# Attention jobs of the third chunk on re-spaced to eight half steps, and the first chunk's jobs put in a written order

## The chip, the cores and the metric

One core of a Trainium2 chip. The metric is the device time of one execution in microseconds (us), lower is better. The kernel before has been timed in three runs, whose median is quoted; one more execution of it was profiled.

## What is computed

Three stages, each feeding the next, all in 32-bit floating point (the reference, cut to what matters):

```python
# q, k, v: 4 batches x 8 heads x 576 positions x 64
mask_plain = (rel >= 0) & (rel < 32)                      # heads 0 to 3
mask_dil = (rel >= 0) & (rel < 128) & (rel % 4 == 0)      # heads 4 to 7
scores = np.where(masks, q @ k^T / 8, -1e9)
attn = np.exp(scores - max); attn /= attn.sum() + 1e-9
x = attn @ v                                              # 2304 tokens x 512
h = x @ w_in;  g = max(h, 0) + alpha * min(h, 0)          # 512 -> 2048
x = g @ w_out                                             # 2048 -> 512
h = x @ w_in2; g = P(h) / (Q(h) + 1e-6)                   # P, Q: small polynomials
out = g @ w_out2
```

The four weight matrices arrive as pairs of 32-bit words (64-bit floats) and are decoded on the chip.

## The kernel before

**Chunks and jobs.** The 2304 tokens are cut into 8 chunks of 288 (number u = 0 to 7). Attention for a chunk is 4 jobs, one for each pair of heads `hp` (pairs 0 and 1 plain, 2 and 3 dilated). `attention_job` (L308) is a generator, and each `yield` ends a step: -1 loads queries and keys (`tq`, `tk`); 0 transposes them on TensorE (L382, L386) into `pq`, `pk`; 1 copies these to `qT`, `kT` on ScalarE (L392, L393); 2 loads the values (`tv`); 3 the scores `ps` on TensorE (L423 dilated, L437 plain); 4 and 7 the row maxima of either half on VectorE (L451, into `pr` and `mx`); 6 and 8 the exponentials on ScalarE with their sums (L459); 9 the division by the sums (L466, L467, and the multiply L469, on VectorE for the first three chunks and on GpSimd after); 10 TensorE turns the probabilities (`pp`, L480); 11 ScalarE copies them out (L486); 12 TensorE multiplies by the values (`px`, L531); 13 ScalarE and VectorE write the high and low part of x (`x1h` L543, `x1l` L545).

**The dense layers.** One step n is one chunk u and one block f of 128 of the 2048 hidden columns, and each n has two half steps, built by `half1` (L830): the first holds the 12 matmuls of h (three products of split numbers for each of 4 blocks, L553), the second the 12 matmuls of y for step n-2 (L727). Between them ScalarE computes `r` (L687), VectorE `larger` (L690), ScalarE the high part of g (L693), VectorE the low part (L696). The list `SEQ` says what n is: n = 0 to 7 is chunk 0 with f = 0 to 7 (weights and x whole, in 32 bits, L670), n = 8 to 15 chunk 1 with the same f, n = 16 to 23 chunk 0 with f = 8 to 15, n = 24 to 31 chunk 1 with these, and then each of chunks 2 to 7 has 16 steps in a row.

**Weight decoding** goes in 36 turns, each with its load (L134 for w_in, L139 for w_out, issued by SyncE), a scaling on ScalarE (`w64_exponent`, L148) and, on VectorE, a sign (L154), an upper (L161) and a lower part (L168), and for some a split (L198, L215, L227). Two buffers hold the raw words (`RAWB`). `PACE` sets how many turns a step n takes in.

**What sets the order.** Chunk 0's jobs, the first decode turns and the first steps of chunk 1's first job are called in the order of the string `HEAD` (L72): a digit is the next step of that job, d, x, j, J, i, h, l are a turn's load, scaling, sign, upper, lower, and split parts, k is a step of chunk 1's first job. From there on the half steps call what tables name: `STEPS` gives for each step of a job its half step after the job's start, `BASES` the starts of a chunk's four jobs relative to the 32 half steps of the chunk before, `ON_PE` which steps go behind that half step's matmuls. The first eight jobs (chunks 1 and 2) have starts of their own, `EARLY`, and denser steps, `EARLY_STEPS`. The scheduler of the framework may still move instructions against this order, except inside `tc.manual_schedule()`. Attention has two PSUM banks, and single buffers for `pr`, `qT`, `kT`, `tq`, `tk`.

```python
att_rest.setdefault(s0 + 2, []).append((i + AHEAD, -1))     # the next job's loads
s0 = EARLY[i] if i < len(EARLY) else i // KD * 2 * NF + BASES[i % KD]
```

Of the kernel before, what the change touches and what calls it, by code (L numbers as in the profile page):

```python
# [22 lines left out]
def tile_attention_moe_moe2(  # L23
# [48 lines left out]
    HEAD = '0d12d30011xj01Ji223301h2300110011xj22223333Jil001101d22010331hlxj220133Ji012301d23k0123hl23xj2323Jidhl'  # L72
# [3 lines left out]
    MANH = ''  # L76
    HPS = (1, 0, 3, 2)
    POOLJ = ()
    SPLIT = True
# [7 lines left out]
    PACE = ((8, 0.75), (16, 0.25), (24, 0.75), (128, 0.22))  # L87
# [190 lines left out]
    def mem_head(nm, dil):  # L278

        if dil:  # L280
            at = {"tq": (0, 0), "tk": (0, 512), "tv": (1, 0), "qT": (1, 512),
                  "kT": (2, 0), "pT": (2, 416), "pr": (3, 0)}
        else:
            at = {"tq": (0, 0), "qT": (0, 384), "tv": (1, 0), "kT": (1, 640),
                  "tk": (2, 0), "pr": (2, 512), "pT": (3, 0)}
# [22 lines left out]
    def attention_job(mem, u, hp, bk, eng=nc.sync, split=False):  # L308
# [5 lines left out]
        first = t0 == 0  # L314
        if dil:
            nb, bq = 4, C1 // 4
            kw = bq if first else bq + W
# [3 lines left out]
            tk = mem("tk", [kw, 2, 4 * D])  # L321

            def load(t, src, back):
                n = t.shape[0]
                s0 = t0 if not back or first else t0 - 4 * W
                eng.dma_start(
                    t,
                    src[b, h0 : h0 + 2, s0 : s0 + 4 * n, :].rearrange(
                        "h (i r) d -> i h (r d)", r=4
                    ),  # L330
                )

            load(tq, q, False)
            load(tk, k, True)

            duo = lambda t, j: t[:, j // 2, (j % 2) * 2 * D : (j % 2 + 1) * 2 * D]
            q_rows, k_rows = bq, kw
        else:


            nb, bq = 3, 96
            groups = ((0, 1, 2), (3, 4))
            rows, span = P, 96
            back = 0 if first else W
# [35 lines left out]
        kn = 4 if dil else nk  # L380
        for j in range(nb):
            nc.tensor.transpose(  # L382
                pq[:, j * q_rows : (j + 1) * q_rows], duo(tq, j), ident[:q_rows, :q_rows]
            )
        for j in range(kn):
            nc.tensor.transpose(  # L386
                pk[:, j * k_rows : (j + 1) * k_rows], duo(tk, j), ident[:k_rows, :k_rows]
            )
        yield
        kT = mem("kT", [P, kn * k_rows])  # L390
        qT = mem("qT", [P, C1])
        nc.scalar.activation(qT, pq[:, :C1], AF.Copy)  # L392
        nc.scalar.activation(kT, pk[:, : kn * k_rows], AF.Copy)  # L393
        yield
        if dil:
            tv = mem("tv", [kw, 2, 4 * D])
            load(tv, v, True)
        else:
            tv = mem("tv", [span, 5, 2, D])
            s0 = t0 - back  # L400
            if first:
                load_one(tv[:, 0], v, s0)
                load(tv[:, 1:], v, s0 + key[1], QS, 4)
            else:
                load(tv, v, s0, QS, 5)
# [8 lines left out]
        def scores():  # L414


            if dil:

                ps[:] = [bk(f"ps{nm}_{g}") for g in range(2)]
                for c in range(nb):  # L420
# [36 lines left out]
        def exponentials(g):  # L457
            for j in groups[g]:
                nc.scalar.activation(  # L459
                    pr[:, j, :], pr[:, j, :], AF.Exp, scale=-1.0,  # L460
                    bias=mx[:, j : j + 1], accum_out=sm[:, j : j + 1],
                )

        def norm(gs):
            s = slice(groups[gs[0]][0], groups[gs[-1]][-1] + 1)
            nc.vector.tensor_scalar_add(sm[:, s], sm[:, s], 1e-9)  # L466
            nc.vector.reciprocal(sm[:, s], sm[:, s])  # L467
            n = s.stop - s.start
            (nc.vector if u < NORM_DVE else nc.gpsimd).tensor_tensor(  # L469
                pr[:, s], pr[:, s],  # L470
                sm[:, s].unsqueeze(2).to_broadcast([rows, n, span]), op=ALU.mult,
# [13 lines left out]
        def turned(g):  # L485
            nc.scalar.activation(  # L486
                pT[:, g * width[0] : g * width[0] + width[g]], pp[g][:span, : width[g]],
                AF.Copy,
            )
# [16 lines left out]
        if split:  # L506
            turn(0)
            yield
            turned(0)
            yield  # L510
        rest = (1,) if split else (0, 1)
        norm(rest)
        yield
        for g in rest:
            turn(g)
        yield
        for g in rest:
# [41 lines left out]
    if True:  # L559
# [27 lines left out]
        def x1_tiles(u):  # L587
            if u == 0:
# [42 lines left out]
        nc.gpsimd.dma_start(alpha_sb, alpha.rearrange("(f p) -> p f", p=P))  # L631


        nc.vector.tensor_scalar(side, alpha_sb, 1.0, -2.0, op0=ALU.is_gt, op1=ALU.mult)
        nc.vector.tensor_scalar_add(side, side, 1.0)
        nc.vector.tensor_tensor(salpha, side, alpha_sb, op=ALU.mult)
        nc.gpsimd.dma_start(ab[:, 0:4], a_in.unsqueeze(0).to_broadcast([P, 4]))
        nc.gpsimd.dma_start(ab[:, 4:6], b_in.unsqueeze(0).to_broadcast([P, 2]))
        def head():
            for s in HEAD:  # L640
                if s in stages:
                    stage(s)
# [414 lines left out]
```

## Time and profile before

| what | before |
|---|---|
| three runs, median (lowest to highest) | 957.85 us (955.93 to 959.39) |
| the profiled execution, its own time | 958.93 us |
| its span in the profile | 957.2 us |
| mean granted TensorE clock | 0.981 of full |
| busy: TensorE, VectorE, ScalarE, GpSimd | 931.6, 663.9, 632.3, 213.3 us |

The span is what the profiler records from the first to the last instruction; 1.7 us of the execution lie around it. The dense layers of attention's chunks end at about 546 us; what follows is the third stage, which has no attention. Four stretches are used below: 0 to 43.4 us (the head: chunk 0's attention until the first `larger`, L690, is done), 43.4 to 139.4 (steps up to n = 23), 139.4 to 181.6 (n = 24 to 31), and 181.6 to 546 (chunks 2 to 7).

### The profile page before, as it was taken

The numbers are of one execution on the slowest core, as the hardware profiler recorded it, in microseconds if no ns is written. First come the engines' busy times: TensorE is split into PE (matmuls) and PEld (weight loads), VectorE is DVE, ScalarE is ACT, GpSimd is POOL, SyncE is SP. The second block draws the span as 40 slices with busy tenths as digits, with TensorE's granted clock in tenths as the row PEclk, the third lists the DMA queues.
The fourth block names the chain that finished last, engine by engine and source line by source line (L and its number), as shares of the span: only waits on it lengthen the run. The fifth ranks groups of instructions, "written<-read, shape, count | busy, mean of one in ns | idle before, by whom it ended". The sixth has DMA issues, their size and how long they took to land.

```text
span 957.2 us, 18319 instructions
## 1 busy us (share of the span) xinstructions
PE 931.6 (97%) x6640; PEld 859.2 (90%) x6640; DVE 663.9 (69%) x1578; ACT 632.3 (66%) x1579; POOL 213.3 (22%) x257
## 2 busy tenths in 40 slices
PE   5898999999999999999999999999999999999998
PEld 4677998999999999999999999999999999999996
DVE  3688996556556556556536698877787777777776
ACT  3788676665564565655636588777777767776775
POOL 2000000010000010000103345444344343443432
PEclk7699999999999999999999999999999999999999
DMA  7666444453644534534145412030020020020000
GB/s 167 184 185 195 143 149 141 137 184 104 194 122 114 190 108 141 160 87 132 47 136 174 153 57 67 0 98 2 20 80 1 34 67 1 34 67 1 34 1 33
DMA packets 93898, 94.39 MB, mean 99 GB/s; under 512 B 40176, under 2 KB 81648, under 8 KB 93808
## 3 DMA queue, kind: packets, MB, share of 16 engines
q1 hardware_dynamic: 87360, 83.78, 28.5%
q0 software_dynamic: 6448, 9.45, 4.0%
q8 instruction: 52, 0.85, 0.4%
q14 instruction: 38, 0.31, 0.1%
HBM read 69.48 MB, written 23.72 MB: 97 GB/s over the span
## 4 chain that ended last, share of the span: by engine, by line
PE 81%; DMA 7%; ACT 6%; DVE 3%; issue 1%; SPq 1%; POOL 0%; POOLq 0%; ACTq 0%; DVEq 0%
PE h L553 38%; PE o L970 20%; PE y L727 16%; DMA raw<-in_moe_w_out_dram 5%; PE px L531 2%; DMA raw<-in_moe_w_in_dram 2%; PE pp L480 1%; ACT hd L459 1%; PE ps L423 1%; PE h L670 1%; ACT raw L148 1%; ACT pr L459 1%; DVE h L690 1%; DVE w L161 1%; PE ps L437 1%
## 5 line engine op out<-in xcount | busy, mean ns | idle before, releaser
L553 PE MATMUL h<-x1h,wl 128*128 128x288 f32 x480 | 146.5, 305 | 1.9 <-ACT g_6h L693 1.6
L553 PE MATMUL h<-x1l,wh 128*128 128x288 f32 x480 | 142.4, 297 | 0.0
L553 PE MATMUL h<-x1h,wh 128*128 128x288 f32 x480 | 141.3, 294 | 0.0
L690 DVE SCALAR_TENSOR_TENSOR h<-h,salpha,r 128x288 f32<-128x288 f32 x128 | 66.9, 523 | 96.6 <-ACT r L687 96.2
L553 PE MATMUL h<-x2h,wl 128*128 128x384 f32 x384 | 130.4, 340 | 0.0
L553 PE MATMUL h<-x2h,wh 128*128 128x384 f32 x384 | 130.0, 339 | 0.0
L553 PE MATMUL h<-x2l,wh 128*128 128x384 f32 x384 | 129.6, 338 | 0.0
L469 POOL TENSOR_TENSOR pr<-pr,sm 128x480 f32<-128x480 f32 (+2 forms) x20 | 24.0, 1198 | 448.3 <-DVE sm L467 382.7
L687 ACT ACTIVATE r<-h,side 128x288 f32<-128x288 f32 x128 | 63.7, 498 | 87.1 <-PE h L553 84.9
L902 POOL TENSOR_SCALAR qq<-hh,babs 128x384 f32<-128x384 f32 x96 | 56.9, 593 | 224.8 <-ACT hh L900 224.7
L905 POOL TENSOR_TENSOR qq<-qq,w 128x384 f32<-128x384 f32 x96 | 97.9, 1019 | 8.3 <-POOL qq L902 0.4
L553 PEld LDWEIGHTS h<-x1h,wl 128*128 128x128 f32 x480 | 90.0, 188 | 5.5 <-ACT g_6h L693 2.1
L553 PEld LDWEIGHTS h<-x1l,wh 128*128 128x128 f32 x480 | 90.2, 188 | 0.8 <-DVE x1l L545 0.5
L553 PEld LDWEIGHTS h<-x1h,wh 128*128 128x128 f32 x480 | 90.2, 188 | 0.1
L900 ACT ACTIVATE hh<-h 128x384 f32<-128x384 f32 x96 | 47.1, 490 | 62.2 <-PE h L553 62.2
L907 DVE TENSOR_TENSOR t<-h,t 128x384 f32<-128x384 f32 x96 | 53.5, 558 | 47.2 <-ACT t L906 46.8
L553 PEld LDWEIGHTS h<-x2h,wl 128*128 128x128 f32 x384 | 72.0, 188 | 4.0
L553 PEld LDWEIGHTS h<-x2l,wh 128*128 128x128 f32 x384 | 72.1, 188 | 3.6
L916 ACT ACTIVATE w<-qq 128x384 f32<-128x384 f32 (+1 forms) x98 | 50.9, 519 | 34.0 <-POOL qq L905 33.9
L553 PEld LDWEIGHTS h<-x2h,wh 128*128 128x128 f32 x384 | 72.0, 187 | 0.0
L924 DVE TENSOR_TENSOR qq<-qq,w 128x384 f32<-128x384 f32 (+1 forms) x98 | 54.2, 553 | 25.0 <-ACT w L919 24.7
L459 ACT ACTIVATE pr<-pr,mx 128x96 f32<-128x96 f32 (+2 forms) x182 | 65.0, 361 | 3.8 <-DVE mx L451 3.8
(379 smaller groups left out, 2558.0 us busy)
## 6 DMA issues: line engine op xcount, KB each, us to landing
raw<-in_moe_w_in_dram SPq DMA_DIRECT2D x32, 512.0 KB
raw<-in_moe_w_out_dram SPq DMA_DIRECT2D x32, 512.0 KB
w2f<-w SPq DMA_DIRECT2D x32, 256.0 KB
w<-w2f SPq DMA_DIRECT2D x16, 512.0 KB
x2h<-x2hi POOLq DMA_DIRECT2D x6, 768.0 KB, 5.1
x2l<-x2lo POOLq DMA_DIRECT2D x6, 768.0 KB, 6.6
out_dram<-o SPq DMA_DIRECT2D x15, 256.0 KB
tq<-in_q_dram SPq DMA_DIRECT2D x28, 72.0 KB
```

Of the source, the lines that this page charges most:

```text
L459: nc.scalar.activation(pr[:, j, :], pr[:, j, :], AF.Exp, scale=-1.0, bias=mx[:, j : j + 1], accum_out=sm[:, j : j + 1],)
L553: nc.tensor.matmul(ph[:, :n], lhsT=w_[:, c * P : (c + 1) * P], rhs=x_[:, c, :], start=(i == 0), stop=(i == 3 * KD - 1),)
L687: nc.scalar.activation(r, h, AF.Identity, scale=sg)
L690: nc.vector.scalar_tensor_tensor(h, h, sa, r, op0=ALU.mult, op1=ALU.max)
L727: nc.tensor.matmul(ys[c][:, :C1], lhsT=w_[:, s], rhs=g_, start=begin and i == 0, stop=end and i == 2,)
L900: nc.scalar.activation(hh, h, AF.Square)
L902: nc.gpsimd.tensor_scalar(qq, hh, babs, 1.0 + 1e-6, op0=ALU.mult, op1=ALU.add)
L905: nc.gpsimd.tensor_tensor(qq, qq, w, op=ALU.add)
L907: nc.vector.tensor_tensor(t, h, t, op=ALU.mult)
L916: nc.scalar.activation(w[:, s], qq[:, s], AF.Abs_reciprocal_sqrt, scale=2.0**-44)
L924: nc.vector.tensor_tensor(qq[:, s], qq[:, s], w[:, s], op=ALU.mult)
L970: nc.tensor.matmul(o2[c][i], lhsT=g_, rhs=w_, start=(f == 0 and j == 0), stop=(f == NF - 1 and j == 2),)
```

## The change

The tables of steps and starts are new. A job of chunks 2 to 7 now starts eight half steps after the one before it (-6, 2, 10, 18), and its four TensorE steps lie at half steps 0, 2, 6 and 12 of the job. Only chunk 1's jobs keep the denser early table. `HEAD` is a new string, which runs under `tc.manual_schedule()`. In chunk 0's jobs query and key loads are issued by SyncE and ScalarE in turn, value loads by GpSimd; the copy of `kT` and of the first half of the turned probabilities goes to VectorE; the exponentials no longer add up their rows, which one VectorE reduction for a job does. The division is one step for both halves. The loads of alpha and its three small VectorE operations come late in the head (`a`).

```diff
-    STEPS = (1, 2, 3, 4, 4, 4, 7, 7, 8, 8, 8, 9, 10, 13)
-    ON_PE = (0, 3, 5, 10, 12)
-    BASES = (-3, 3, 9, 15)
+    STEPS = (0, 1, 1, 2, 3, 3, 3, 3, 4, 5, 6, 7, 12, 13)
+    ON_PE = (0, 3, 10, 12)
+    BASES = (-6, 2, 10, 18)
...
-    EARLY = (-6, -2, 1, 5, 40, 48, 55, 58)
+    EARLY = (-6, -2, 1, 5)
...
-    HEAD = '0d12d30011xj01Ji223301h2300110011xj22223333Jil001101d22010331hlxj220133Ji012301d23k0123hl23xj2323Jidhl'
+    HEAD = (
+        '0123dd01010101000001111232212033322220010021333312132xjJid21'
+        '2323hlxjJid333hlaxjJidkhl'
+    )
...
-    PACE = ((8, 0.75), (16, 0.25), (24, 0.75), (128, 0.22))
+    PACE = ((8, 0.85), (16, 0.25), (24, 0.75), (128, 0.22))
...
-        nc.scalar.activation(kT, pk[:, : kn * k_rows], AF.Copy)
+        if head:
+            nc.vector.tensor_copy(kT, pk[:, : nk * kw])
+        else:
+            nc.scalar.activation(kT, pk[:, : nk * kw], AF.Copy)
...
-                    bias=mx[:, j : j + 1], accum_out=sm[:, j : j + 1],
-                )
+                nc.scalar.activation(
+                    pr[:, j, :], pr[:, j, :], AF.Exp, scale=-1.0, bias=mx[:, j : j + 1],
+                    **({} if head else dict(accum_out=sm[:, j : j + 1])),
+                )
+        def norm():
+            if head:
+                nc.vector.tensor_reduce(
+                    out=sm, in_=pr, op=ALU.add, axis=mybir.AxisListType.X
+                )
...
+            if head and g == 0:
+                nc.vector.tensor_copy(t, pp[g][:span, : width[g]])
+            else:
+                nc.scalar.activation(t, pp[g][:span, : width[g]], AF.Copy)
...
-                0, hp, hb, nc.gpsimd if hp in POOLJ else nc.sync, SPLIT,
-            )
-            for hp in HPS
+                0, hp, hb, (nc.sync, nc.scalar)[i % 2], nc.gpsimd, True,
+            )
+            for i, hp in enumerate(HPS)
...
-        nc.gpsimd.dma_start(alpha_sb, alpha.rearrange("(f p) -> p f", p=P))
+        def sides():
+            nc.gpsimd.dma_start(alpha_sb, alpha.rearrange("(f p) -> p f", p=P))
...
+                elif s == "a":
+                    sides()
...
-        if MANH:
-            with tc.manual_schedule():
-                head()
-        else:
+        with tc.manual_schedule():
             head()
```

**The order of instructions: SyncE's queue at the start.** A name is a tile: `hd` holds the head's tiles of a job (`hd_1` is the job of pair 1), `raw` a turn's raw weights. Before:

```order
L353 DMA hd_1_0_92<-in_q_dram 96x3x64 x2
L353 DMA hd_1_2_94<-in_k_dram 96x3x64 x2
L134 DMA raw_153<-in_moe_w_in_dram 128x4x256
L353 DMA hd_0_0_96<-in_q_dram 96x3x64 x2
L353 DMA hd_0_2_98<-in_k_dram 96x3x64 x2
L326 DMA hd_3_0_100<-in_q_dram 72x2x256
L326 DMA hd_3_0_100<-in_k_dram 72x2x256
L134 DMA raw_161<-in_moe_w_in_dram 128x4x256
L326 DMA hd_2_0_104<-in_q_dram 72x2x256
L326 DMA hd_2_0_104<-in_k_dram 72x2x256
```

and now:

```order
L352 DMA hd_1_0_92<-in_q_dram 96x3x64 x2
L352 DMA hd_1_0_92<-in_k_dram 96x3x64 x2
L329 DMA hd_3_0_100<-in_q_dram 72x2x256
L329 DMA hd_3_0_100<-in_k_dram 72x2x256
L134 DMA raw_157<-in_moe_w_in_dram 128x4x256
L134 DMA raw_159<-in_moe_w_in_dram 128x4x256
```

The loads of pairs 0 and 2 have left this queue (they are ScalarE's first instructions now), and both weight loads stand behind the queries and keys.

**VectorE in the head.** `w_0` and `w_1` are the decoded weights of turns 0 and 1. Before, the engine begins with

```order
L154 TENSOR_SCALAR w_0_186<-raw_153 128x512
L161 SCALAR_TENSOR_TENSOR w_0_186<-raw_153,w_0_186 128x512
L168 SCALAR_TENSOR_TENSOR w_0_195<-raw_153,w_0_186 128x512
L634 TENSOR_SCALAR side<-alpha_sb 128x16
L635 TENSOR_SCALAR side<-side 128x16
L636 TENSOR_TENSOR salpha<-side,alpha_sb 128x16
L154 TENSOR_SCALAR w_1_268<-raw_161 128x512
L161 SCALAR_TENSOR_TENSOR w_1_268<-raw_161,w_1_268 128x512
L168 SCALAR_TENSOR_TENSOR w_1_311<-raw_161,w_1_268 128x512
L451 ISA hd_1_2_94,mx_1_221<-ps_1_1_224,masks_122 128x96
```

and now these turns stand behind all maxima of chunk 0, at rows 71 to 81:

```order
L469 TENSOR_TENSOR hd_3_3_103<-hd_3_3_103,sm_3_259 72x576
L154 TENSOR_SCALAR w_0_382<-raw_157 128x512
L161 SCALAR_TENSOR_TENSOR w_0_382<-raw_157,w_0_382 128x512
L168 SCALAR_TENSOR_TENSOR w_0_385<-raw_157,w_0_382 128x512
L487 COPY hd_3_2_102<-pp_3_0_371 72x288
L464 TENSOR_REDUCE sm_2_278<-hd_2_3_107 72x8
L467 TENSOR_SCALAR sm_2_278<-sm_2_278 72x8
L468 RECIPROCAL sm_2_278<-sm_2_278 72x8
L469 TENSOR_TENSOR hd_2_3_107<-hd_2_3_107,sm_2_278 72x576
L154 TENSOR_SCALAR w_1_418<-raw_159 128x512
L161 SCALAR_TENSOR_TENSOR w_1_418<-raw_159,w_1_418 128x512
L168 SCALAR_TENSOR_TENSOR w_1_421<-raw_159,w_1_418 128x512
```

The two decodes have moved from ahead of the first maxima to behind the third and the fourth job's division.

**ScalarE at step n = 27 of chunk 1**, where decode turn 18 is scaled (`raw_2004` before, `raw_1853` now) and chunk 2's jobs run (`pr_2`, `pr_3`). Before:

```order
L687 ACTIVATE r_1_11_1922<-h_1_11_1909,side 128x288
L393 ACTIVATE kT_2_1935<-pk_2_1926 128x288
L693 ACTIVATE g_1_11h<-h_1_11_1909,side 128x288
L148 ACTIVATE raw_2004<-raw_2004 128x512
L459 ACTIVATE pr_2_1956,sm_2_1958<-pr_2_1956,mx_2_1957 72x72 x5
L687 ACTIVATE r_1_12_1987<-h_1_12_1974,side 128x288
L459 ACTIVATE pr_2_1956,sm_2_1958<-pr_2_1956,mx_2_1957 72x72 x3
L693 ACTIVATE g_1_12h<-h_1_12_1974,side 128x288
```

and now:

```order
L457 ACTIVATE pr_3_1973,sm_3_1975<-pr_3_1973,mx_3_1974 72x72 x7
L686 ACTIVATE g_1_10h<-h_1_10_1957,side 128x288
L534 ACTIVATE x1h_1577<-px_2_2038 128x4x72
L680 ACTIVATE r_1_11_2035<-h_1_11_2022,side 128x288
L148 ACTIVATE raw_1853<-raw_1853 128x512
L686 ACTIVATE g_1_11h<-h_1_11_2022,side 128x288
L680 ACTIVATE r_1_12_2082<-h_1_12_2069,side 128x288
L489 ACTIVATE pT_3_2047<-pp_3_0_2085 72x288
```

The exponentials of the job at hand stood behind the scaling and now stand ahead of it; the job is pair 3's, where it was pair 2's.

## Rows read from the trace of the kernel before

**Rows 1.** By stage: length; busy PE, PEld, DVE, ACT, POOL; clock, DMA share, GB/s.

```profile
0.00:43.40 43.40, 29.38 (x258) 22.98 (x258) 19.62 (x94) 22.64 (x81) 4.93 (x17) 0.65 0.68 167
43.40:139.40 96.00, 92.53 (x702) 80.03 (x701) 86.33 (x199) 73.52 (x188) 0.00 (x0) 1.00 0.54 170
139.40:181.60 42.20, 39.86 (x385) 37.03 (x384) 24.81 (x90) 25.46 (x86) 0.00 (x0) 0.96 0.46 132
181.60:546.00 364.40, 363.19 (x3262) 350.55 (x3263) 208.05 (x601) 210.99 (x613) 41.09 (x34) 1.00 0.45 137
```

**Rows 2.** Timeline of TensorE in the head: start, us, line, tile, idle before and releaser.

```profile
6.24 0.41 PE L382 MATMUL pq<-ident,hd 96*128 96x96 f32 x3
...
14.83 0.74 PE L386 MATMUL pk<-ident,hd 96*128 96x96 f32 x3 [5.86 <-DMA hd<-in_k_dram]
```

**Rows 3.** Timeline of SyncE's queue in the head: start and length of an issue.

```profile
4.27 0.99 SPq L353 DMA_DIRECT2D hd<-in_k_dram  x2
...
7.87 3.21 SPq L326 DMA_DIRECT2D hd<-in_k_dram  x1
```

**Rows 4.** The DMA view from 6 to 12 us: packets, MB, share of 16 engines.

```profile
q1 hardware_dynamic: 1529, 0.73, 53.3%
q0 software_dynamic: 104, 0.01, 23.4%
```

**Rows 5.** Timeline of ScalarE in the head.

```profile
20.40 0.47 ACT L393 ACTIVATE hd<-pk 128x288 f32<-128x288 f32 x1
20.87 0.38 ACT L459 ACTIVATE hd<-hd,mx 128x96 f32<-128x96 f32 x1
...
39.78 0.68 ACT L543 ACTIVATE x1f<-px 128x288 f32<-128x288 f32 x1 [1.53 <-PE px L531]
```

**Rows 6.** Timeline of VectorE, from 31 to 49 us.

```profile
31.05 1.29 DVE L168 SCALAR_TENSOR_TENSOR w<-raw,w 128x512 int32<-128x512 int32 x2
...
43.03 0.53 DVE L690 SCALAR_TENSOR_TENSOR h<-h,salpha,r 128x288 f32<-128x288 f32 x1 [4.23 <-ACT r L687]
43.47 0.25 DVE L451 CUSTOM_DVE_ANT_0 pr<-ps,masks 128x96 f32<-128x96 f32 x1
...
44.35 0.69 DVE L154 TENSOR_SCALAR w<-raw 128x1024 int32<-128x1024 int32 x1
45.08 1.23 DVE L161 SCALAR_TENSOR_TENSOR w<-raw,w 128x1024 int32<-128x1024 int32 x1
46.22 0.17 DVE L466 TENSOR_SCALAR sm<-sm 128x5 f32<-128x5 f32 x1
...
47.71 0.65 DVE L469 TENSOR_TENSOR pr<-pr,sm 128x480 f32<-128x480 f32 x1
48.27 0.69 DVE L168 SCALAR_TENSOR_TENSOR w<-raw,w 128x512 int32<-128x512 int32 x1
```

**Rows 7.** A weight load, from SyncE's issue to ScalarE's scaling.

```profile
51.15 0.38 SPq L139 DMA_DIRECT2D raw<-in_moe_w_out_dram  x1
...
57.53 1.14 ACT L148 ACTIVATE raw<-raw 128x1024 f32<-128x1024 f32 x1 [0.44 <-DMA raw<-in_moe_w_out_dram]
```

**Rows 8.** Timeline of TensorE from 165 to 170 us.

```profile
165.35 0.67 PE L480 MATMUL pp<-ident,pr 72*72 72x72 f32 x8 [2.03 <-DVE pr L469]
...
166.10 0.44 PE L727 MATMUL y<-g_11l,wh 128*128 128x288 f32 x1
...
169.25 0.35 PE L727 MATMUL y<-g_11h,wh 128*128 128x288 f32 x1
```

**Rows 9.** Timeline of ScalarE ahead of it: the scaling of turn 18.

```profile
159.85 0.67 ACT L148 ACTIVATE raw<-raw 128x512 f32<-128x512 f32 x1 [3.12 <-DMA raw<-in_moe_w_in_dram]
```

**Rows 10.** Timeline of TensorE where chunk 2 begins.

```profile
178.22 0.72 PE L531 MATMUL px<-pT,tv 72*64 72x72 f32 x16
178.87 0.40 PE L553 MATMUL h<-x1h,wl 128*128 128x288 f32 x1
...
180.43 0.40 PE L553 MATMUL h<-x1l,wh 128*128 128x288 f32 x1
180.89 0.71 PE L437 MATMUL ps<-kT,qT 64*64 64x96 f32 x20
```

More of the change, by code (lines that the diff above doesn't have):

```diff
@@ L305, in mem_head, with attention_job @@
         return f
-    def attention_job(mem, u, hp, bk, eng=nc.sync, split=False):
+    def attention_job(mem, u, hp, bk, eng=nc.sync, eng_v=nc.sync, head=False):
         b, t0 = divmod(u * C1, S)
@@ L314, in attention_job @@
         first = t0 == 0
+        back = 0 if first else (4 * W if dil else W)
         if dil:
-            nb, bq = 4, C1 // 4
-            kw = bq if first else bq + W
+            nq = nk = 4
+            bq = C1 // 4
+            kw = bq + back // 4
             groups = ((0, 1, 2, 3), (4, 5, 6, 7))
@@ L321, in attention_job, with load @@
             tk = mem("tk", [kw, 2, 4 * D])
-            def load(t, src, back):
-                n = t.shape[0]
-                s0 = t0 if not back or first else t0 - 4 * W
+            duo = lambda t, j: t[:, j // 2, (j % 2) * 2 * D : (j % 2 + 1) * 2 * D]
+            def load(t, src, s0, eng):
                 eng.dma_start(
                     t,
-                    src[b, h0 : h0 + 2, s0 : s0 + 4 * n, :].rearrange(
+                    src[b, h0 : h0 + 2, s0 : s0 + 4 * t.shape[0], :].rearrange(
                         "h (i r) d -> i h (r d)", r=4
@@ L396, in attention_job @@
             tv = mem("tv", [kw, 2, 4 * D])
-            load(tv, v, True)
+            load(tv, v, t0 - back, eng_v)
         else:
@@ L400, in attention_job @@
             s0 = t0 - back
+            n1 = 1 if first else 0
             if first:
-                load_one(tv[:, 0], v, s0)
-                load(tv[:, 1:], v, s0 + key[1], QS, 4)
-            else:
-                load(tv, v, s0, QS, 5)
+                eng_v.dma_start(
+                    tv[:, 0],
+                    bass.AP(
+                        v.tensor, ((b * H + h0) * S + s0) * D,
+                        [[D, span], [S * D, 2], [1, D]],
+                    ),
+                )
+            for h in range(2):
+                eng_v.dma_start(
+                    tv[:, n1:, h, :],
+                    bass.AP(
+                        v.tensor, ((b * H + h0 + h) * S + s0 + key[n1]) * D,
+                        [[D, span], [QS * D, 5 - n1], [1, D]],
+                    ),
+                )
         yield
@@ L419, in scores @@
                 ps[:] = [bk(f"ps{nm}_{g}") for g in range(2)]
-                for c in range(nb):
+                for c in range(4):
                     for g in range(2):
@@ L459, in exponentials @@
                 nc.scalar.activation(
-                    pr[:, j, :], pr[:, j, :], AF.Exp, scale=-1.0,
-                    bias=mx[:, j : j + 1], accum_out=sm[:, j : j + 1],
-                )
[L464 to L468, printed above, removed]
+                    pr[:, j, :], pr[:, j, :], AF.Exp, scale=-1.0, bias=mx[:, j : j + 1],
+                    **({} if head else dict(accum_out=sm[:, j : j + 1])),
+                )
+        def norm():
+            if head:
+                nc.vector.tensor_reduce(
+                    out=sm, in_=pr, op=ALU.add, axis=mybir.AxisListType.X
+                )
+            nc.vector.tensor_scalar_add(sm, sm, 1e-9)
+            nc.vector.reciprocal(sm, sm)
             (nc.vector if u < NORM_DVE else nc.gpsimd).tensor_tensor(
-                pr[:, s], pr[:, s],
-                sm[:, s].unsqueeze(2).to_broadcast([rows, n, span]), op=ALU.mult,
+                pr, pr, sm.unsqueeze(2).to_broadcast([rows, nblk, span]), op=ALU.mult
             )
@@ L485, in turned @@
         def turned(g):
[L486 to L489, printed above, removed]
+            t = pT[:, g * width[0] : g * width[0] + width[g]]
+            if head and g == 0:
+                nc.vector.tensor_copy(t, pp[g][:span, : width[g]])
+            else:
+                nc.scalar.activation(t, pp[g][:span, : width[g]], AF.Copy)
         scores()
@@ L505, in attention_job @@
         pT = mem("pT", [span, sum(width)])
[L506 to L512, printed above, removed]
+        norm()
         yield
-        for g in rest:
+        for g in range(2):
             turn(g)
         yield
-        for g in rest:
+        for g in range(2):
             turned(g)
```

71 lines of the change are left out of this document (24 added, 47 removed).

## The prediction

> **What bounds the kernel now.** I read the busy time and clock by stage first, then the timelines of the stages that are not full. In the long stretch from 181.6 us TensorE has its full clock (2.4 GHz) and is busy for 363.19 of 364.40 us [rows 1]: 1.2 us is all that better spacing can give back there. The reserve lies ahead of it. The head takes 43.4 us with TensorE busy for 29.4 at a clock of 0.65. From 43.4 to 139.4 us TensorE idles for 3.5 us, and VectorE is busy for 86.33 of 96.0: this stage goes by weight decoding and attention on VectorE, 9.7 us above its own work. From 139.4 to 181.6 us TensorE idles for 2.3 us, and the clock of 0.96 says that part of the rest ran at half speed (1.2 GHz) [rows 1].
>
> The timelines say why. In the head the first job's queries are turned at 6.24 us, but the second job's keys hold TensorE up for 5.86 us, until 14.83 [rows 2]; their loads were issued at 4.27, and SyncE's last key load left the queue only at 7.87 + 3.21 = 11.08 [rows 3]. Between 6 and 12 us the 104 small packets of the software queue (alpha's loads) take 23.4% of the 16 DMA engines for 0.01 MB [rows 4]. Chunk 0's x is complete at 39.78 + 0.68 = 40.46 [rows 5]. In the third stage ScalarE waits 3.12 us for turn 18's weights [rows 9] with the exponentials queued behind; TensorE then waits 2.03 us for the normalised `pr`, and its matmuls take 0.44 us until 169.25, where 0.35 begins the return to 0.29, and the stretch's clock is 0.96 [rows 1, 8]. So the clock was at its lower level after this wait for some 3.9 us, from 165.35 to 169.25.
>
> **The change, part by part.**
>
> *The head.* The eight query and key loads leave from two queues, ahead of any weights, and alpha's packets go late, so I take all four jobs' keys to be there when needed and start VectorE's chain at about 7 us, just behind the first turn [rows 2]. Its work until chunk 0's x is complete: 26 maxima at (44.35 - 43.47)/5 = 0.176 us [rows 6], 4.6; eight copies taken from ScalarE at 0.45 (ScalarE's own take 0.47 [rows 5]), 3.6; four divisions at 0.65 for the multiply, 0.3 for two small operations (0.17 each) [rows 6], and an estimated 0.65 for the new reduction, which reads as many elements as the multiply, 6.4; two decodes of half a turn, each (0.69 + 1.23 + 1.29)/2 = 1.6 [rows 6], 3.2. That is 17.8, with some 4 for waits between engines 22, so x is complete at about 29 instead of 40.46.
>
> That gain does not reach the next stage whole. Turns 0 and 1 were decoded first and now end at about 23 and 27, as they stand behind three and four divisions. There are two raw buffers, so turn 2's load waits for turn 0. A load takes 57.53 - 51.15 = 6.4 us to the scaling, this 1.14 [rows 7], the decode 3.2: 10.7 in all. Turn 2 ends at 33.7, turn 3 at 37.7, turn 4 at 44.4; it ended at 48.27 + 0.69 = 48.96 [rows 6]. Chunk 1's first maxima stand behind turn 4 now and start at about 44.5 rather than 43.47 [rows 6]. **The head by itself: 0**, but at the same moment turn 4 (3.2) and three `larger` (1.5) more are done.
>
> *43.4 to 139.4 us.* VectorE loses these 4.7 us. It takes over the earlier half of chunk 2's attention, two jobs that move from half steps 40 and 48 to 26 and 34: each 0.9 for maxima, 0.35 for small operations, 0.65 for the multiply and an estimated 0.45 for x's low part, as many elements as a copy, 2.35, or 4.7 for both. Its work stays at 86.3, TensorE's falls with the h and y done earlier. What may go is the idle 9.7: all of it (-9.5) if the earlier turns keep VectorE fed; none, with the 1 us of the later start and two falls of the clock at 1.9 like the one below (+5). I take **-4**, nearer the end that turn 4 shows: it is 4.6 us earlier, and the steps n = 4 to 8 each wait for a turn.
>
> *139.4 to 181.6 us.* The exponentials now stand ahead of turn 18's scaling, so its wait no longer holds `pr`; what is late next is g of n = 27, behind the same scaling. The 2.03 us [rows 8] go. The 3.9 us at the lower clock cost half of themselves, 1.9. TensorE also gets about 1.25 jobs fewer: a job costs it about 2.4 (scores 0.7, `px` 0.65 [rows 10], the two transposing steps an estimated 0.5 each, a little under the 0.67 that one took at the lower clock [rows 8]), so 3.0. That is 6.9; **-5.5** since the close `px` may take a microsecond. Bounds: -4 (g_11's wait stays) and -7.
>
> *From 181.6 us on.* Two-apart steps can win back at most 0.9 of the idle 1.2 [rows 1]. Against it, the last job's `px` now stands two half steps before the chunk's first h, where it stood seven before. Twelve matmuls take about 1.6 (178.87 to 180.43 for the first eleven) and `px` 0.65 [rows 10], so 2.25 us lie between its start and h. In the order, at two of five boundaries (chunks 3 and 5) VectorE has five maxima, a full decode, two small operations and g's low part ahead of `larger` and x's low part. With the last three at `larger`'s 0.5 [rows 6] that is 0.9 + 3.2 + 0.35 + 1.5 = 6.0 from the end of `ps`, where TensorE wants it after 1.6 + 1.6 + 0.65 + 1.6 = 5.5: 0.5 lost twice. Together **0**, bounds -1 and +5.
>
> The copies moved to VectorE, the exponentials without sums and the late `side` operations lie in the head, behind the chain above; without that cover each costs its own 0.1 to 0.5 us. GpSimd's value loads are hidden, as values are used only by `px`, a third of the head later.
>
> Sum: 0 - 4 - 5.5 + 0 = -9.5. The profiled execution took 958.93 (span 957.2, 1.7 around it), which gives 949.4. It stands 1.08 above the median of 957.85, so I forecast **948.4** for the median.
>
> **A rule against the head's part.** The trace shows what the page "DMA: Bandwidth & Descriptors" of the Trainium skill, section "Issuing engines are not separate DMA queues", states: loads from different engines run on the same 16 DMA engines, and starting them from several engines saves issue time alone. Here one queue's issues of 0.99 us with a landing ten later [rows 2, 3] at a share of 53.3 + 23.4% [rows 4] agree in part. By it the sum would be that of the second rival.
>
> **The rivals.**
>
> 1. *VectorE's idle vanishes.* The third stage, the head and the end as above, the second stage at its floor, -9.5: -15 in all, **942.9**. For it: 4.7 us of work less ahead of n = 4. Against it: the idle also comes from ScalarE's `r`, which stays, 4.23 us at one place [rows 6].
> 2. *The two queues share what one had.* Query and key loads of four jobs are 1.15 MB; at the head's 167 GB/s [rows 1] that is 6.9 us, and if they interleave, the first job's land with the last, near 11 instead of 6. Everything in the head is 4 later, and chunk 1's maxima start at 48: -5.5, **952.4**.
> 3. *No change.* The second stage gives nothing back, as the later start (1) and the closer jobs in two PSUM banks stop TensorE and the clock falls twice: +5 instead of -4, so -0.5, **957.4**.
> 4. *Slower: the late `px`.* If x's parts come later than the 2.25 us behind `px`'s start at every boundary, TensorE waits; waits of about 2 us were followed by half speed [rows 8], one of 0.1 was not [rows 10]. At the price of that place, 2.0 + 1.9 at each of five boundaries is 19.5, so +10: **967.9**. It decides from a wait of about 2 us on, that is when ScalarE's five exponentials (0.38 each [rows 5], 1.9) and a scaling of 1.14 [rows 7] come ahead of the copy with nothing of them done. Against it: in the order they start 3.2 us earlier, at `ps`; and when chunk 2 began directly behind its `px`, it lost 0.1 us [rows 10].
>
> That the order is not what the tables say is no rival: the placed steps stand where they were put.
>
> **How the numbers follow.** Forecast 0.50 (its own range 944 to 953), rival 1 0.13, rival 2 0.14, rival 3 0.12, rival 4 0.11. About 0.3% (2.9 us) is what a measurement tells from no change: faster is below 955.0, slower above 960.7. Faster: nearly all of the forecast, rival 1 and most of rival 2, 0.72; same: rival 3 and the rest, 0.15; slower: rival 4 and a little of rival 3, 0.13. The range from 941 to 958 leaves out rival 4, a part of rival 3 and the far half of rival 1's spread.
>
> **What would show it.** `px` of the last job of chunk 0 copied near 29 us; turn 4's end near 44; the first `larger` of n = 23 near 135 instead of 139.45; no wait of `pp` on `pr` near 160 and a clock of 1.00 there; no idle of over 1 us of TensorE where chunks 3 to 7 begin. It is wrong if the second job's keys land after 11, if VectorE's busy share from 44 us to n = 23 stays at 90%, or if `h` waits for x's low part at each boundary.

## The result: slower by 1.2%, and the profile after

The changed kernel takes 969.93 us (median of 4 runs, 967.65 to 971.61) where the kernel before takes 958.62 in the runs beside it: a ratio of 1.0121, with a 95% interval of 1.0088 to 1.0153. The forecast was 948.4, with a range of 941 to 958. The profiled execution took 971.61, its span is 969.7 us, the mean granted clock 0.976.

A ruler for both traces is the start of VectorE's `larger` for each step n (L690 before, L683 now), 128 rows in either trace. In us:

| step n | before | after, less before | the forecast's term, and what came |
|---|---|---|---|
| 0 | 43.03 | -9.3 | head: chunk 0's x earlier, as forecast |
| 4 | 64.91 | -13.8 | |
| 5 | 69.30 | -2.5 | 11 of the 14 us are gone here already |
| 8 | 89.99 | +1.0 | the first step of chunk 1: all of it gone |
| 23 | 139.45 | +9.1 | head and second stage: -4 forecast |
| 32 | 181.59 | +0.1 | third stage: -5.5 forecast, -9.0 came |
| 64 | 308.38 | +1.1 | |
| 68 | 325.34 | +7.3 | chunk 4's start |
| 104 | 467.02 | +11.1 | chunk 6's start at n = 96 to 99 |
| 127 | 547.85 | +13.0 | the rest: 0 forecast, +12.9 came |

So at n = 32 the two kernels stand side by side, and the whole loss comes in the stretch where TensorE was full before. The windows by stage (length; busy PE, PEld, DVE, ACT, POOL; clock, DMA share, GB/s), which answer to [rows 1]:

```profile
0.00:47.90 47.90, 38.27 (x299) 29.32 (x300) 29.64 (x101) 21.41 (x54) 10.36 (x25) 0.75 0.69 166
47.90:148.50 100.60, 92.89 (x742) 80.60 (x741) 87.30 (x226) 77.35 (x214) 0.00 (x0) 0.95 0.53 167
148.50:181.60 33.10, 33.10 (x309) 32.05 (x308) 20.25 (x68) 20.79 (x63) 0.99 (x1) 1.00 0.52 149
181.60:560.80 379.20, 369.28 (x3267) 355.56 (x3266) 206.01 (x590) 206.13 (x605) 41.31 (x34) 0.99 0.43 132
```

The third stage has become what was forecast: TensorE is busy for all 33.10 us at full clock. The last stretch has 9.9 us of idle TensorE, where the one of [rows 1] had 1.2, and a clock below 1. What TensorE waited for in it (engine, operation, releaser: total, times, longest):

```profile
PE y L720 <- DVE y_3l L751: 3.2, 3, 2.0
PE pp L479 <- POOL pr L469: 3.0, 2, 1.5
PE pq L368 <- ACT pT L489: 2.3, 1, 2.3
```

None of these is the wait that the slower rival named. All lie where a chunk's dense layer has just ended and its result is copied out of PSUM, the "spill" (`y_0h` to `y_3h` on ScalarE, L750, the low parts on VectorE, L751, and their stores). The next chunk's y needs the same four banks, so its matmuls wait for `y_3l`. Around n = 67, in chunk 4's first steps, TensorE shows:

```profile
319.00 0.66 PE L720 MATMUL y<-g_1h,wl 128*128 128x288 f32 x3
321.17 0.75 PE L479 MATMUL pp<-ident,pr 128*96 128x128 f32 x5 [1.50 <-POOL pr L469]
324.25 0.74 PE L368 MATMUL pq<-ident,tq 72*128 72x72 f32 x4 [2.33 <-ACT pT L489]
...
325.67 0.44 PE L720 MATMUL y<-g_0l,wh 128*128 128x288 f32 x1
...
329.03 0.34 PE L544 MATMUL h<-x1h,wh 128*128 128x288 f32 x1
```

and ScalarE, where the exponentials, x's copy, a turn's scaling (L148) and one `pT` stand ahead of `y_3h`:

```profile
316.36 0.50 ACT L680 ACTIVATE r<-h,side 128x288 f32<-128x288 f32 x1 [1.03 <-PE h L544]
317.62 0.38 ACT L457 ACTIVATE pr<-pr,mx 128x96 f32<-128x96 f32 x1 [0.76 <-DVE mx L449]
...
319.43 0.39 ACT L534 ACTIVATE x1h<-px 128x288 fp32r<-128x288 f32 x1
322.72 1.10 ACT L148 ACTIVATE raw<-raw 128x1024 f32<-128x1024 f32 x1 [2.90 <-DMA raw<-in_moe_w_out_dram]
323.72 0.47 ACT L489 ACTIVATE pT<-pp 96x384 f32<-96x384 f32 x1
324.10 0.40 ACT L750 ACTIVATE y_3h<-y 128x288 fp32r<-128x288 f32 x1
```

VectorE follows with `y_3l` and, queued behind it, the low part of g that frees the bank for the next h:

```profile
324.52 0.46 DVE L751 TENSOR_TENSOR y_3l<-y,y_3h 128x288 fp32r<-128x288 f32 x1 [4.21 <-ACT y_3h L750]
324.90 0.51 DVE L689 SCALAR_TENSOR_TENSOR g_1l<-h,side,g_1h 128x288 fp32r<-128x288 f32 x1
```

TensorE stands for 1.50 and 2.33 us, and then runs matmuls of 0.44 us, its lower clock, until 329.03. The profile puts these two waits down to `pr` and `pT`, steps of a job; in TensorE's order these stand ahead of the matmuls that need `y_3`'s bank or the low part of g, so a late `y_3h` leaves TensorE nothing else to do.

Two queues meet at `y_3h`. On ScalarE the scaling waits 2.90 us for its weights, with `pT` and `y_3h` behind it. On SyncE the same turn's loads, 1 MB, stand just ahead of the store of `y_0h`:

```profile
314.35 0.45 SPq L134 DMA_DIRECT2D raw<-in_moe_w_in_dram  x1
314.85 0.86 SPq L139 DMA_DIRECT2D raw<-in_moe_w_out_dram  x1
...
316.28 0.49 SPq L752 DMA_DIRECT2D x2hi<-y_0h  x1
```

`y_3h` is written into a buffer that this store has to empty first. By the semaphore updates in the trace the store landed at 323.65, 7.4 us after its issue, and `y_3h` started 0.45 us later. In the spills of chunks 2 to 6 of all thirteen traces, 65 in all, no `y_3h` starts before `y_0h`'s store has landed; the least distance is 0.08 us. In the kernel before, at the same place, a scaling stood ahead of `y_3h` too and waited for its load too, but the second of its loads had been issued 3.75 us before the store, which landed 1.9 us after its issue, at 315.45:

```profile
309.85 0.57 SPq L139 DMA_DIRECT2D raw<-in_moe_w_out_dram  x1
313.60 0.33 SPq L759 DMA_DIRECT2D x2hi<-y_0h  x1
```

```profile
315.11 1.14 ACT L148 ACTIVATE raw<-raw 128x1024 f32<-128x1024 f32 x1 [0.94 <-DMA raw<-in_moe_w_out_dram]
...
316.43 0.40 ACT L757 ACTIVATE y_3h<-y 128x288 fp32r<-128x288 f32 x1
```

At n = 99 of the change the scaling waits for no load and ends at 453.55, and it is the store that `y_3h` waits for; it was issued at 448.48, behind the turn's load of 447.52, and landed at 454.46:

```profile
454.54 0.41 ACT L750 ACTIVATE y_3h<-y 128x288 fp32r<-128x288 f32 x1 [1.00 <-DMA x2hi<-y_0h]
```

The head answers to [rows 2, 5, 6] so. TensorE's last transpose of chunk 0's keys, ScalarE's last copy of x with the scaling of turn 2 behind it, and chunk 1's first maxima on VectorE:

```profile
9.24 0.44 PE L368 MATMUL pk<-ident,hd 72*128 72x72 f32 x4
```

```profile
30.97 0.68 ACT L534 ACTIVATE x1f<-px 128x288 f32<-128x288 f32 x1 [2.06 <-PE px L522]
31.44 1.13 ACT L148 ACTIVATE raw<-raw 128x1024 f32<-128x1024 f32 x1
```

```profile
46.71 1.29 DVE L168 SCALAR_TENSOR_TENSOR w<-raw,w 128x512 int32<-128x512 int32 x2
47.92 0.25 DVE L449 CUSTOM_DVE_ANT_0 pr<-ps,masks 128x96 f32<-128x96 f32 x1
```

x is complete at 31.65 instead of 40.46, but turn 4 ends at 48.0, and chunk 1's attention begins 4.4 us later than before.

### The profile page after: what moved, and what is told of

It reads as the page before. It is cut to its first block, busy times and chain, and to the rows that moved or that the text cites. A ratio compares the mean times of both kernels' runs of the same rounds, so it can differ in the third digit from the quotient of the medians.

```text
span 969.7 us, 18289 instructions
## 1 busy us (share of the span) xinstructions
PE 938.4 (97%) x6640; PEld 864.3 (89%) x6640; DVE 666.5 (69%) x1578; ACT 624.4 (64%) x1545; POOL 218.8 (23%) x265
## 4 chain that ended last, share of the span: by engine, by line
PE 79%; DMA 5%; DVE 5%; ACT 3%; issue 1%; POOL 0%; SPq 0%; POOLq 0%; ACTq 0%; DVEq 0%
PE h L544 38%; PE o L963 20%; PE y L720 16%; DMA raw<-in_moe_w_out_dram 4%; PE px L522 1%; DMA x2hi<-y_0h 1%; DVE w L168 1%; DVE w L161 1%; PE ps L421 1%; PE pp L479 1%; PE pk L368 1%; PE pq L368 1%; ACT r L680 1%; DMA yp<-y1p 0%; PE ps L435 0%
## 5 line engine op out<-in xcount | busy, mean ns | idle before, releaser
L544 PE MATMUL h<-x1h,wl 128*128 128x288 f32 x480 | 143.5, 300 | 0.9 <-ACT x1h L534 0.6
L683 DVE SCALAR_TENSOR_TENSOR h<-h,salpha,r 128x288 f32<-128x288 f32 x128 | 66.8, 522 | 108.3 <-ACT r L680 108.3
```

What stands on the lines that cost most here:

```text
L544: nc.tensor.matmul(ph[:, :n], lhsT=w_[:, c * P : (c + 1) * P], rhs=x_[:, c, :], start=(i == 0), stop=(i == 3 * KD - 1),)
L683: nc.vector.scalar_tensor_tensor(h, h, sa, r, op0=ALU.mult, op1=ALU.max)
```

## The experiments

Theory A: the loss is an order on ScalarE. The change moves the decode turns by a fraction of a turn (three turns in the head for four, 0.85 for 0.75 a step up to n = 8: 9.8 turns by n = 8 for 10.0, and 0.2 of a turn is two half steps at 0.22 a step), so that in the spills of chunks 3 and 5 a scaling and the exponentials come ahead of `y_3h`. A second reading of the same meeting is an order on SyncE: the turn's loads come just ahead of the stores that empty `y_3h`'s buffer. Moving the turns moves both, so e1, e2 and e4 do not tell them apart. Theory B, the rival of either: the new spacing of the jobs itself costs the time. Theories C and D are on the losses at n = 115 and at n = 8.

**e1: the turns moved clear of the spills.**

```diff
-    PACE = ((8, 0.85), (16, 0.25), (24, 0.75), (128, 0.22))
+    PACE = ((8, 0.85), (16, 0.25), (24, 0.75), (25, 0.62), (128, 0.22))
```

> The changed kernel with its decode turns from n = 25 on moved some four half steps earlier (one extra 0.40 of a turn at n = 24), so that in every chunk's spill ScalarE copies y_3 directly behind r, with no scaling of a turn and at most one job's exponentials ahead of it. Theory A (spill: the new chunk's y waits for the old chunk's y_3, which stands on ScalarE behind a turn's scaling whose load is late): the losses at n = 67 (about 7 us) and n = 99 (about 5 us) go, 958 to 961 us. Theory B (the new spacing of the jobs costs it, wherever the turns fall): 967 to 972.

960.51 us, 1.0012 [0.9990, 1.0034] of before. The ruler stands at -2.4 for n = 64, -1.0 for n = 67, -2.5 for n = 104: both losses are gone, with the jobs where the change put them. B is out for these two losses.

**e2: the turns moved by one more half step**, 0.72 in place of 0.62. (That is earlier than in e1; the expectation has the direction wrong, though not the spills that it names, which were read from the order of the instructions.)

> The changed kernel with its turns one half step later than in e1 (0.50 of a turn extra at n = 24): the scaling and the exponentials now stand ahead of y_3 in the spills of chunks 2 and 4, and no longer in those of chunks 3 and 5. Theory A: losses of 5 to 7 us each at n = 51 and n = 83 and none at n = 67 and 99, 966 to 972 in all. Theory B: 967 to 972 as well, but with the losses where they were, at n = 67 and 99.

978.25 us, 1.0177 [1.0147, 1.0208]. The losses came where A said, which is also where the loads now stand just ahead of the stores: from n = 50 to 51 the ruler jumps by 7.0 and from 82 to 83 by 7.3; at 67 it rises by 2.8 and gives 1.5 back at 68, at 99 by 0.4. ScalarE in chunk 2's spill:

```profile
261.71 1.10 ACT L148 ACTIVATE raw<-raw 128x1024 f32<-128x1024 f32 x1 [2.40 <-DMA raw<-in_moe_w_out_dram]
...
263.08 0.40 ACT L750 ACTIVATE y_3h<-y 128x288 fp32r<-128x288 f32 x1
```

`y_0h`'s store was issued at 256.69, behind loads of 255.15 and 255.59, and landed at 262.40, 0.7 us ahead of this copy. The time was above the 966 to 972 expected. From n = 48 to 53 the ruler rises by 5.9 and from 80 to 84 by 6.9, as expected; another 4.5 came between n = 72 and 80, where h once waits 3.0 us for a low part of g, and why was not followed up.

**e3: the new spacing alone**, in the kernel before: its head and turns, with the changed `STEPS`, `ON_PE`, `BASES` and `EARLY`.

> The kernel before with the new tables of steps and starts alone (old head, old turns). No scaling stands ahead of y_3 in any spill but that of chunk 5, where it comes ahead of r. Theory A: no loss at n = 67, at most 2 us at n = 99, and 2 at n = 115 from the later last px: 957 to 963. Theory B: 967 to 972.

957.93 us, 0.9978 [0.9958, 0.9997]: no loss at n = 67 or 99, as A expected. The spacing is by itself worth some 2 us (0.3 to 4 by the interval). Its ruler is -3.1 at n = 32, -4.7 at n = 112 and -1.0 at n = 116; the 3.8 us lost there are more than the 2 expected.

**e4: the new head alone**, the changed kernel with the old tables of spacing.

> The changed kernel with the old tables of steps and starts (new head and its turns). In the spills of chunks 3 and 5 exponentials, qT, kT and pT (and a scaling in chunk 5's) stand ahead of y_3. Theory A: losses of 3 to 7 us at n = 67 and n = 99, none of 2 at n = 115, 962 to 970. Theory B: 952 to 959.

970.14 us, 1.0095 [1.0064, 1.0126]: as slow as the change, without the new spacing. Here the ruler rises by 6.6 from n = 66 to 67, but only 2.2 us of it last from n = 64 to 68, and 1.7 from n = 96 to 104, less than expected; 4.7 us came between n = 32 and n = 64, which was not followed up. In chunk 3's spill no scaling stands ahead of `y_3h`, but exponentials and `pT` of two jobs do, waiting for TensorE and VectorE:

```profile
324.45 0.76 ACT L489 ACTIVATE pT<-pp 96x384 f32<-96x384 f32 x2 [1.80 <-PE pp L479]
326.27 0.37 ACT L457 ACTIVATE pr<-pr,mx 128x96 f32<-128x96 f32 x1 [1.06 <-DVE mx L449]
...
327.36 0.39 ACT L750 ACTIVATE y_3h<-y 128x288 fp32r<-128x288 f32 x1
```

So no scaling ahead of `y_3h` is needed. The turn's weights are not out by this: their loads of 320.35 and 320.79 stand just ahead of `y_0h`'s store on SyncE, issued at 321.46, which landed at 327.21, 0.15 us ahead of `y_3h`.

**e9 and e11: the spill called first.** The strictest test leaves every turn and every step of a job at its half step and changes only the place at which a half step calls the spill.

```diff
+            if n > 32:
+                for fn in later.pop((n, half), []):
+                    fn()
             while pace[0] >= 1:
                 pace[0] -= 1
                 tick()
             attn(2 * n + half, False)
```

> The changed kernel with nothing moved but the place at which a half step calls the old chunk's spill: ahead of the turn and of the jobs' steps (from n = 33 on). Turns and spacing stay at their half steps, and y_3 follows r on ScalarE in the spills of chunks 3 and 5 (in chunk 2's a scaling stands ahead of it now). Theory A (order on ScalarE): the losses at n = 67 and 99 fall from 8 and 5 us to under 2 each, 958 to 964, with at most 5 us lost at n = 51. If it is the turn's load that collides with the stores, wherever y_3 stands: 967 to 972.

971.01 us, 1.0121 [1.0075, 1.0168]: a miss in the total. The jumps at 67 and 99 did go (the ruler is 5.7 at n = 64, 6.1 at 67, 7.3 at 104), but 5.2 new us were lost from n = 32 to 48, 3.9 of them from n = 33 to 36, where the spill of chunk 1, which reads a partial result back, now came first too. Hence e11, with `n > 52` in place of `n > 32`:

> The changed kernel with the spill called first from n = 53 on alone, so that the spills of chunks 1 and 2 stand as in the change, and those of chunks 3 and 5 have y_3 directly behind r, with all turns and steps of jobs at the half steps of the change. Theory A (order on ScalarE): n = 64 as in the change (about +1), no loss of over 1.5 us at n = 67 and 99, 2 to 3 at n = 115, 959 to 964. If the load of the turn itself, or the jobs' spacing, costs the 13 us: 967 to 972.

962.89 us, 1.0053 [1.0030, 1.0076]. The ruler is 0.0 at n = 64, 0.4 at 67, 1.3 at 104 and 3.2 at 127. ScalarE has `y_3h` right behind r, the scaling waits later for the same load, with nothing behind it that TensorE wants, and TensorE is busy for all of the 35 us (windows as above, in a fence of their own):

```profile
315.29 0.50 ACT L680 ACTIVATE r<-h,side 128x288 f32<-128x288 f32 x1 [1.16 <-PE h L544]
315.69 0.40 ACT L750 ACTIVATE y_3h<-y 128x288 fp32r<-128x288 f32 x1
...
323.22 1.13 ACT L148 ACTIVATE raw<-raw 128x1024 f32<-128x1024 f32 x1 [1.43 <-DMA raw<-in_moe_w_out_dram]
```

```profile
310.00:345.00 35.00, 35.00 (x326) 33.76 (x326) 19.69 (x60) 20.40 (x62) 2.57 (x2) 1.00 0.51 160
```

With turns and jobs called at the half steps of the change, the order of turn and spill alone takes 10.0 - 1.4 = 8.6 us of the change's loss between n = 64 and n = 104 away in these traces (6.5 us by the ratios of the whole times). So the loss is the meeting of turn and spill, and the spacing of the jobs is out again as its cause. It does not show that the order on ScalarE is the cause, since the edit changes SyncE's order as well: the first four stores of the spill now leave ahead of the turn's loads.

```profile
313.48 0.35 SPq L752 DMA_DIRECT2D x2hi<-y_0h  x1
...
316.83 0.46 SPq L134 DMA_DIRECT2D raw<-in_moe_w_in_dram  x1
317.34 0.56 SPq L139 DMA_DIRECT2D raw<-in_moe_w_out_dram  x1
```

`y_0h`'s store landed here 2.1 us after its issue, at 315.59, and at n = 99 as well after 2.1 us. With the change's order on SyncE a `y_3h` directly behind r would still have waited for the store, until 323.65 and 454.46: by these traces ScalarE's order alone could give back 0.45 and 0.1 us at the copy. With the change's order on ScalarE and the stores first, `y_3h` would still stand behind the scaling, which ends at 323.82 and 453.55: nothing at n = 67 and 1.0 us at n = 99. So either order alone makes `y_3h` late, as far as the traces tell. No run changed one queue without the other, and the price of each is not shown.

**e5 and e6: the loss at n = 115.** In the change, TensorE waits 2.02 us there for `y_3l` without a job or a turn near it. ScalarE's `y_3h` waits until `y_0h` has been stored, since both use one pool of buffers:

```profile
512.12 0.40 ACT L750 ACTIVATE y_0h<-y 128x288 fp32r<-128x288 f32 x1
...
516.35 0.41 ACT L750 ACTIVATE y_3h<-y 128x288 fp32r<-128x288 f32 x1 [2.04 <-DMA x2hi<-y_0h]
```

and GpSimd's first loads of the third stage had been issued, behind attention's last `px`, 7.5 us before the first of these copies:

```profile
504.61 0.79 POOL L817 DMA_DIRECT2D x2h<-x2hi  x1 [12.84 <-PE px L522]
505.39 0.77 POOL L818 DMA_DIRECT2D x2l<-x2lo  x1
```

Together with SyncE's three weight loads of 512 KB issued at 504.11 they are 3 MB, and in the DMA view the 16 engines are busy from 505 until about 516 us. In the change these loads start 9.7 us ahead of the `larger` of n = 114, in the kernel before 17.7, as its last `px` came earlier. Theory C puts chunk 7's jobs back on the old tables:

```diff
+    LSTEPS, LBASES = (1, 2, 3, 4, 4, 4, 7, 7, 8, 8, 8, 9, 10, 13), (-3, 3, 9, 15)
...
-        s0 = EARLY[i] if i < len(EARLY) else i // KD * 2 * NF + BASES[i % KD]
+        s0 = EARLY[i] if i < len(EARLY) else i // KD * 2 * NF + (LBASES if i // KD == NC1 - 2 else BASES)[i % KD]
```

(and `LSTEPS` likewise), in e1 for e5 and in e3 for e6.

> e1 with chunk 7's four jobs on the old steps and starts, so that attention's last px comes five half steps (8 us) earlier. Theory C (the third stage's first 3 MB of loads wait for attention's memory and meet chunk 6's y stores at n = 115): the 3 us that e1, e2 and e3 lose at n = 115 go, 956 to 959. Otherwise 960 to 962.

958.90 us, 0.9993 [0.9971, 1.0015]. The ruler is 0.2 at n = 114 and 0.2 at n = 116, where e1 has -2.5 and +1.1: the loss is gone in the trace. By the ratios e5 is 1.8 us faster than e1, and their intervals overlap. ScalarE's copy now starts 0.06 us behind r:

```profile
502.94 0.50 ACT L681 ACTIVATE r<-h,side 128x288 f32<-128x288 f32 x1 [0.68 <-PE h L545]
503.51 0.41 ACT L751 ACTIVATE y_3h<-y 128x288 fp32r<-128x288 f32 x1
```

> e3 (old head, new spacing) with chunk 7's jobs on the old tables. Theory C: no loss at n = 115, e3 less 3.5: 953 to 956. Otherwise 957 to 960.

957.72 us, 0.9980 [0.9961, 1.0000]: above what was expected. Here too the step at n = 115 is gone (-0.6 on either side), but the median is that of e3. e3 and e6 are one program up to chunk 7, and their profiled executions stand 3.3 us apart at n = 32 already: so far the head scatters from one execution to the next. By the ratios chunk 7 on the old tables is worth 1.8 us in e5, nothing in e6 and 3.5 in e8 (against e7): theory C is shown in the traces at n = 115, its worth in whole times is not.

**e7: chunk 1's first loads early.** The last of the head's 14 us are gone at n = 8, the first step that needs chunk 1's attention, and this attention begins no earlier than before: its loads are called behind turn 4's load, which waits for turn 2's buffer and was issued at 37.42. Theory D moves the call in e1:

```diff
-        '0123dd01010101000001111232212033322220010021333312132xjJid21'
-        '2323hlxjJid333hlaxjJidkhl'
+        '0123dd01010101000001111232212033322220010021333312132xjJikd21'
+        '2323hlxjJid333hlaxjJidhl'
```

> e1 with chunk 1's first query and key loads called ahead of the third decode turn's load in the head's order instead of behind the fifth's. Theory D (the head's gain is lost since chunk 1's attention, which n = 8 waits for, starts no earlier than before): chunk 1's first maxima come some 10 us earlier, near 33 us, n = 8 by 5 to 9 us, and the time is 951 to 956. If the stage to n = 8 goes by decode turns or by VectorE's work: n = 8 moves by under 2 us, 959 to 962.

954.98 us, 0.9966 [0.9938, 0.9994]. Chunk 1's first maxima come at 34.03 instead of 47.65 in e1:

```profile
34.03 0.26 DVE L449 CUSTOM_DVE_ANT_0 pr<-ps,masks 128x96 f32<-128x96 f32 x1 [4.11 <-PE ps L435]
```

n = 8 is 3.9 us earlier than in e1, less than the 5 to 9 expected. But this place scatters: in the six traces with the old call (the change, e1, e2, e5, e9, e11) the ruler at n = 8 is between -1.1 and +1.4, in the three with the early call (e7, e8, e10) between -5.7 and -5.0, on the mean 5.7 us apart. The time follows by some 4.4 us (ratios 1.0012 and 0.9966). So D holds for part of the lost gain. The lead of chunk 0's steps is not kept along with it: at n = 4 the ruler is -1.7 in e7, where e1 has -14.0. What holds the rest was not tried.

**e8: e5 and e7 together**, and **e10: the same without e1's moved turns, with e9's order instead.**

> e5 and e7 together. Theories C and D: 948 to 953. C alone: 956 to 959. D alone: 951 to 956.

952.89 us, 0.9929 [0.9904, 0.9954]: faster than both kernels, by 0.7% than the one before. The ruler is -5.2 at n = 127, with no lasting step at 67, 99 or 115.

> e9 together with chunk 1's loads early and chunk 7 on the old tables, without the moved turns of e1: all of theories A, C and D by another way. 949 to 956; over 960 if calling the spill first does not take the place of moving the turns.

959.71 us, 0.9995 [0.9970, 1.0020]: a miss. It stands at -7.5 at n = 32 and -0.8 at n = 48, the loss that e9 has there, 5.4 us of it from n = 33 to 36; calling the spill of chunk 1 first gives the gain back.

## Why the prediction was wrong

**The head's own term (0) was too small.** The loads went as forecast: all keys are turned by 9.7 us, and x is complete at 31.65 for a forecast 29. Rival 2, in which the first job's loads are slowed by sharing, is out: the first queries were turned at 5.91 us, earlier than before. The Trainium skill's page "DMA: Bandwidth & Descriptors", section "Issuing engines are not separate DMA queues", says that several issuing engines save issue time alone. Issue time was saved here: SyncE's last key load left at 3.67 + 0.30 where it had left at 11.08 [rows 3]. More than that was gained: the second job's keys were issued 2.5 us earlier (1.73 for 4.27) and turned 8.2 us earlier (6.66 for 14.83); the weight loads and alpha's packets no longer stand before or beside them, and no run parts these causes. The turns were taken too short: turn 2's scaling stood on ScalarE behind the last copy of x (30.97, row above), so turn 2 ended at 37.35 and not 33.7, and turn 4 at 48.0, not 44.4. So chunk 1's first maxima came 4.4 us later than before, where 1 us was forecast.

**Head and second stage (-4; +9.1 came).** A failed step is "what may go is the idle 9.7", the assumption that the stage goes by VectorE's amount of work: VectorE was busy for 87.30 of 100.60 us, which leaves it 13.3 us idle. The 14 us that chunk 0's steps were ahead were gone by n = 8, which waits for chunk 1's attention, a chain of four jobs that began 4.4 us later; e7 shows a part of it, as its earlier start moved n = 8. The two jobs of chunk 2 were taken as 4.7 us of VectorE work that lies beside the rest. With the new spacing the ruler loses 6.0 us in e3 and 7.5 in the change between n = 15 and n = 23, where these jobs now run; e4, with the old spacing and the new head, loses 1.1.

**The third stage (-5.5; -9.0 came)** was right in its mechanism: no wait for `pr`, clock 1.00, and the moved jobs' work gone. Its size holds what the second stage paid for. Over both, e3 gains 2.6 us from n = 15 to n = 32: most of the moved work is moved, not saved. Up to n = 32 the forecast was -9.5 and +0.1 came, 9.6 of the 22.5 us by which the ruler misses the forecast.

**From 181.6 us on (0, bounds -1 and +5; +12.9 came)** is the step that failed most. The prediction looked at one place, x's late parts, and for each boundary listed what stands ahead of them. It took no row for the other thing that happens two steps later, the spill, and it did not carry `PACE` beyond the head: "0.85" and three head turns shift every later turn by two half steps. In the spills of chunks 3 and 5 this put the turn's loads just ahead of y's stores on SyncE, and exponentials and x's copy, besides the scaling that stood there before, ahead of `y_3h` on ScalarE. `y_0h`'s store then landed after 7.4 and 6.0 us, where it had taken 1.9 and 1.7, and `y_3h` and TensorE behind it waited. e1 and e2 show that the loss goes where the turns go, and e11 that the order of turn and spill makes 8.6 of its 10.0 us; which of the two queues costs how much stays open. The late last `px`, which was costed for h alone, also released the third stage's loads late, ahead of the same kind of store: 2 us in the change, 3 to 3.6 in e1.

**The slower rival** had the size nearly (967.9), by luck: it summed five boundaries and a wait for x's parts, and the losses came at three, from the spill. In the whole trace h waited for x's high part for 0.6 us, and a `px` for a low part for 0.2:

```profile
PE h L544 <- ACT x1h L534: 0.6, 2, 0.4
...
PE px L522 <- DVE x1l L536: 0.2, 1, 0.2
```

What it had right is how a wait is priced: 3.8 us of waits at n = 67 were followed by matmuls of 0.44 us until 329.03.

## What to carry to other kernels

A change to one table can move a periodic piece of work elsewhere by a fraction of its period: list, for every recurring event (here the turns' scalings), what it now meets at each place where banks or buffers change hands, and read on each in-order queue what stands ahead of the instruction that frees them. That includes the queue that issues stores: a copy out of PSUM can wait for the buffer that an earlier store still holds, and a store just behind 1 MB of loads held it for 7.4 us here. Calling the spill ahead of the turn put both the stores ahead of the loads and the copy ahead of the scaling, and that was enough for chunks 3 and 5; for chunk 1, whose spill reads a partial result back, 3.9 us were lost in e9. And a head that ends earlier is worth nothing until the first consumer of the next chunk has been started earlier as well.

## What was not expected of the hardware

A store's landing time depends on what else is under way. The 144 KB of `y_0h` landed 1.7 us after the issue at best (e5: issued at 501.69, landed at 503.42), after 3.7 us among the 3 MB of the third stage's loads (512.55 to 516.27), and after 7.4 and 6.0 us just behind a turn's loads.

And TensorE's lower clock did not follow from the length of one wait. After split waits of 1.15 and 1.45 us at 54.55 and 56.72 the window from 58 to 64 us has a granted clock of 0.59, with TensorE busy throughout. A single wait of 2.02 us at 517.30 was followed by matmuls at the upper level, and one of 2.03 us in the kernel before by matmuls at the lower level [rows 8]. What decides between the last two was not found.

```profile
54.55 0.71 PE L435 MATMUL ps<-kT,qT 64*64 64x96 f32 x20 [1.15 <-ACT kT L378]
56.72 1.33 PE L522 MATMUL px<-pT,tv 96*64 96x56 f32 x20 [1.45 <-DVE mx L449]
...
517.30 0.40 PE L720 MATMUL y<-g_0h,wl 128*128 128x288 f32 x1 [2.02 <-DVE y_3l L751]
```

```profile
512.00:522.00 10.00, 7.98 (x60) 7.75 (x60) 5.04 (x10) 5.41 (x13) 1.80 (x2) 1.00 0.66 192
58.00:64.00 6.00, 6.00 (x22) 4.63 (x21) 4.79 (x9) 3.84 (x14) 0.00 (x0) 0.59 0.56 165
```

The first fence is TensorE's timeline of the change, the second its windows, in the columns of the result's section.
